# Two layers of attention and S4D convolution: staging the output weights elsewhere, new due times, one planner cost, tied additions and a reordered pool

## The chip, the cores and the metric

The kernel runs on one core of one Trainium2 chip. The metric is device time in microseconds (us) of one execution. Five engines work in parallel, each through its own instructions in their order: TensorE (PE), VectorE (DVE), ScalarE (ACT), GpSimd (POOL) and SyncE (SP). In this kernel SP issues most of the transfers and POOL the rest. The granted clock is the share of TensorE's full clock that the profile shows.

## The reference, cut to what matters

```python
def _A_ref(x, wqkv, wo):                     # S=2048, D=640, H=32 heads of 20
    qkv = (x @ wqkv)...                      # q, k, v per head
    scores = jnp.einsum("bhqd,bhkd->bhqk", q, k) * (Dh ** -0.5)
    p = _softmax(scores, axis=-1)
    o = jnp.einsum("bhqk,bhkd->bhqd", p, v)
    return o... @ wo
def _B_ref(u, log_A_real, A_imag, C_real, C_imag, log_dt, D_skip):
    dt = jnp.exp(log_dt)
    A = -jnp.exp(log_A_real) + 1j * A_imag   # 640 channels x 128 states
    C = (C_real + 1j * C_imag) * dt[:, None]
    P = jnp.exp((A * dt[:, None])[:, :, None] * pos[None, None, :])
    K = 2.0 * jnp.einsum("dn,dnl->dl", C, P).real      # one kernel of 2048 steps per channel
    ... y = irfft(rfft(u) * rfft(K))[:L]               # causal convolution
    return y + u * D_skip
x = x + _A_ref(_layernorm(x), ...)
x = x + _B_ref(_layernorm(x), ...)
x = x + _A_ref(_layernorm(x), ...)
x = x + _B_ref(_layernorm(x), ...)
```

## The kernel before, in words

The program is two layers, each an attention and then an output projection with the convolution. Both layers use the same weights and the same kernel K, so the generator of K and its transform run once, in layer 1.

**Attention.** The work is cut into 32 turns (8 groups of 4 heads by 4 blocks of 512 queries), each of 16 steps kt of 128 keys. A step makes two score tiles S on TensorE (`S<-qop,kop`), two exponentials of 128x1024 on ScalarE (`pt<-S`), and the products with the values (`pa<-pt,V`). At a turn's end VectorE gathers the block in `oc`, POOL sends its row of sums through DRAM (`dn<-oc`, `dr<-dn`), VectorE inverts them (`dr`), POOL spreads them again (`dn<-dr`, `db<-dn`), VectorE multiplies `oc` by `db`, and POOL stores `ot<-oc`. The very last block takes a way without DRAM (`m<-oc,dsel`, a reciprocal of `db`). A group change (turns 3, 7, 11 and so on) needs the next heads' operands, which SP loads (`kop<-ks`, `qop<-qs`, `qop<-qm`).

**What fills the gaps.** In layer 1 the same stretch also holds the q, k, v projections of the later groups (`m<-xh,wh`, emptied by VectorE into `qc`, split into `qhi`, `qlo`, stored to `qs` and `ks`; their weights `ws` split into `wh`, `wl`) and the generator `kgen` of K. For each of its 20 blocks POOL loads powers (`kpw<-wd`), VectorE's `expand` makes a table of them (`kpw`, `ktab`, `kwc`, `kwb`, `kdif`), VectorE makes the factors `ka` and `kb`, TensorE contracts them (`m<-kb,ka`, L335), VectorE empties `ko`, and POOL stores `kd<-ko`.

**What sets the order.** The program is written by a planner: class `Plan` keeps an estimated time of TensorE, ScalarE and VectorE (`plan.pe`, `plan.act`, `plan.dve`). Every VectorE operation adds its cost to `plan.dve`; a wait for a transfer adds nothing. `weave` emits the next piece of `kgen` where the plan has room, and the list `later` holds small steps, among them loads, each with a due time. While `plan.keep` is set, `tie` makes each instruction follow the one before on its engine; elsewhere a scheduler chooses the order, and `tie` is used where one operation shall follow another. Every engine then executes its list in order.

**The end of the first attention.** `end_jobs` runs when projections and generator are done. It calls `prefetch`, which opens the pools of the output projection, loads the output weights and puts the remaining loads into `rest`; these get due times from `plan.pe` on. `woh` and `wol` are the rounded half and the remainder of the weights:

```python
with tc.tile_pool(name="wos", bufs=NCT, side="right") as ws:
    for ct in range(NCT):
        wt = ws.tile([P, D], F32, name="wot")
        sy.dma_start(wt, wo[ct * P:ct * P + P, :])
        ge.tensor_copy(woh[:, ct, :], wt)
        ge.tensor_sub(wol[:, ct, :], wt, woh[:, ct, :])
```

**Output projection 1 and the kernel transform.** TensorE multiplies the rows `otl` (split into `oh`, `ol` by ScalarE and VectorE) with the weights into `po`, and VectorE adds `po` to `x` and takes statistics. `ktransform` runs between: for each of five blocks of 128 channels it loads `kl<-kd`, adds the skip to the first column (`kl<-kl,skip`, VectorE), transposes (`pkt<-ident,kl`), splits into `ktrh` and `ktrl`, multiplies by `e1s` (`pkx`), transposes and scales into `kxt` and makes `kn`. `kl0` holds its buffers; `kl0[3]`, called `kx1` or `kx`, is the one into which `pkx` is emptied.

**The convolution** (`ssm`) goes by rows of 128 positions: layer norm (`va`, `lt`, `rs`, `nb`, `u`, `uhx`, `ulx`), a transform (`psx<-uhx,e1s`, emptied into the pair `x1`, which the profile calls `x`, by a cast on ScalarE and a subtraction on VectorE), the product with the factors `ka`, `kb`, which SP loads, and the way back, for which SP loads `eb`. Buffers come from pools; where a pool takes memory that an earlier tile still holds, its first use waits for that tile.

Of the kernel before, what the change touches and what calls it, by code (L numbers as in the profile page):

```python
# [11 lines left out]
F32 = mybir.dt.float32  # L12
F32R = mybir.dt.float32r
F16 = mybir.dt.float16
# [73 lines left out]
def mha_s4d_kernel(ctx, tc, x_in, wqkv, wo, lar, aim, cr, ci, ldt, dsk,  # L88
# [109 lines left out]
    def kgen():  # L198
# [69 lines left out]
        def expand(k, w, tab, dif):  # L268

            while slow and slow[0][0] <= k:  # L270
                slow.pop(0)[1]()
            bs = slice(k * BC, k * BC + BC)
            lo = [tab[:, r, :, 0:24].rearrange("p d (g k) -> p d g k", k=8) for r in range(2)]
            hi = [tab[:, r, :, 24:28] for r in range(2)]
            for r in range(2):
                ve.tensor_mul(w[:, r], w[:, r], w[:, 2])
                a3 = w[:, r, 0:9, :].rearrange("p (g k) d -> p d g k", k=3)
                ve.tensor_copy(lo[r][:, :, :, 1:3], a3[:, :, :, 0:2])
                ve.tensor_copy(lo[r][:, :, :, 4:5], a3[:, :, :, 2:3])
                ve.tensor_copy(hi[r][:, :, 0:1], ld["ci" if r else "cr"][:, bs].unsqueeze(2))  # L280
                yield
            cm = [ld[n][:, bs].unsqueeze(2).to_broadcast([P, BC, 3]) for n in ("cr", "ci")]
            yield from cmul([a[:, :, 1:4] for a in hi], [w[:, r, 9:12, :].rearrange("p n d -> p d n") for r in range(2)], cm, [P, BC, 3], "kwc")
            yield from cmul([a[:, :, :, 3] for a in lo], [a[:, :, :, 1] for a in lo],
                            [a[:, :, :, 2] for a in lo], [P, BC, 3], "kwc")
            w4 = [a[:, :, :, 4:5].to_broadcast([P, BC, 3, 3]) for a in lo]
            yield from cmul([a[:, :, :, 5:8] for a in lo], [a[:, :, :, 1:4] for a in lo], w4, [P, BC, 3, 3], "kwb")
            ve.tensor_add(tab[:, 2], tab[:, 0], tab[:, 1])
            yield
            ve.tensor_sub(dif, lo[1][:, :, 0:3:2], lo[0][:, :, 0:3:2])  # L290
# [139 lines left out]
    def attention(x, stats):  # L430
# [521 lines left out]
        def end_jobs():  # L952

            while filler[0] is not None:
                while slot():
                    pass
                weave(1)
            if not first_layer:
                wx = sm.tile([P, 2], F32, name="wx")
                ve.reduce_max(wx[:, 0:1], wm, axis=AX.X)  # L960
                ge.partition_all_reduce(wx[:, 1:2], wx[:, 0:1], P, bass.bass_isa.ReduceOp.max)

                def bounds():
                    ve.tensor_max(flag[:, 0:1], flag[:, 0:1], wx[:, 1:2])
                    ve.reciprocal(wx[:, 0:1], wx[:, 1:2])
                    ve.tensor_scalar_mul(wx[:, 0:1], wx[:, 0:1], 2.0 ** -4)
                    ve.tensor_max(flag[:, 0:1], flag[:, 0:1], wx[:, 0:1])
                later.append((plan.pe + 6.0, bounds))
            qc_.close()
            if not first_layer:  # L970
                xpools.pop().__exit__(None, None, None)
            rest = []
            made = prefetch(x, rest)
            later.extend((plan.pe + 8.0 + (3.0 if first_layer else 4.0) * n, f) for n, f in enumerate(rest))
            later.sort(key=lambda e: e[0])
            return made

# [179 lines left out]
    def prefetch(x, rest):  # L1157
# [16 lines left out]
        if rest:  # L1174
            kl0[:] = [w1.tile([P, L], F32, name="kl"), w1.tile([P, NCT], F32, name="skip"),
                      w1.tile([P, 2, 32], F32, name="f2"), w1.tile([P, 4, NI // 2, 4, 32], F32, name="kx1"),
                      *(w1.tile([P, NI, P], F16, name=f"ktr{n}") for n in "hl"),
                      *(w1.tile([P, 4, 4, P], F32, name=f"kxt{n}") for n in range(2))]
            late[:] = [w1.tile([P, P], F32, name="dsel")]

            def small():
                sy.dma_start(kl0[1], dsk)
                sy.dma_start(late[0], c_dn)
                sy.dma_start(kl0[2], c_f2.rearrange("p (s m) -> p s m", s=2))
            rest[1:1] = small, lambda: load_kl(0)
            with tc.tile_pool(name="wos", bufs=NCT, side="right") as ws:
                for ct in range(NCT):
                    wt = ws.tile([P, D], F32, name="wot")
                    sy.dma_start(wt, wo[ct * P:ct * P + P, :])
                    ge.tensor_copy(woh[:, ct, :], wt)  # L1190
                    ge.tensor_sub(wol[:, ct, :], wt, woh[:, ct, :])
            rest.pop(0)()
            return x, c, woh, wol, c.enter_context(tc.tile_pool(name="wo2", bufs=2, side="right"))
        w2 = c.enter_context(tc.tile_pool(name="wo2", bufs=2, side="right"))
# [46 lines left out]
    def ktransform(e1):  # L1241

        c = ExitStack()
        c2 = c.enter_context(tc.tile_pool(name="f2", bufs=2))
        kl, skip, f2, x1, hi, lo, *xts = kl0

        def by_time(b, h):

            if h == 0:
                tie(ve.tensor_add(kl[:, 0:1], kl[:, 0:1], skip[:, b:b + 1]), None if b else late[1])  # L1250
            klv = kl.rearrange("d (p i) -> d i p", i=NI)
            for i4 in (2 * h, 2 * h + 1):
                pt = pst("X", [P, 4, P], F32, tag="X", name="pkt")
# [18 lines left out]
        def block(b):  # L1272

            def turned(t, xt, h):
                for q in (2 * h, 2 * h + 1):
                    pt = pst("X", [P, 4, P], F32, tag="X", name="pkt")
                    for g in range(4):
                        transpose(pt[:, g, :], of_group(x1, 16 * t + 4 * q + g), ident)
                    if q % 2:
                        ve.tensor_scalar_mul(xt[:, q], pt, ksc[:, 1:2])  # L1280
                    else:
                        se.activation(xt[:, q], pt, AF.Copy, scale=ksc[:, 1:2])

# [103 lines left out]
    def ssm(x, uh, ul, consts, last):  # L1387
# [18 lines left out]
        e1, f2, id16, fa = consts  # L1406
        with ExitStack() as c:
            c1 = c.enter_context(tc.tile_pool(name="s1", bufs=1))
            c2 = c.enter_context(tc.tile_pool(name="s2", bufs=2))
            c3 = c.enter_context(tc.tile_pool(name="s3", bufs=3))  # L1410
            order = {}

            def at(name, made):
# [36 lines left out]
                return px  # L1450

            def factors(m, ch):
                ka = c1.tile([P, 512], F32, bufs=5, name="ka")
                kb = c3.tile([P, 512], F32, name="kb")
                for t, src in ((ka, kha), (kb, khb)):
                    at("sp", sy.dma_start(t.rearrange("p (q k) -> p q k", k=P), src[m][:, ch]))
                return ka, kb

            def product(px, ka, kb, alone):
                t2 = c1.tile([P, 512], F32, name="t2")  # L1460
                at("dve", ve.stream_shuffle(t2, px, SWAP))
                at("dve", ve.tensor_mul(ka, px, ka))
                for f, *a in (("tensor_mul", kb, t2, kb), ("tensor_add", ka, ka, kb)):
# [35 lines left out]
                return add, after  # L1499

            def new_x1():
                return [c2.tile([P, 4, NI // 2, 4, 32], F16, name=f"x1{k}") for k in range(2)]

            x1 = new_x1()
            for i2 in range(8):
# [5 lines left out]
            for n in range(NQ + 15):  # L1511
# [3 lines left out]
                if n < NQ:  # L1515
                    if q == 0 and b:
                        x1 = nxt
                    if n % 4 == 0:
                        xt = c1.tile([P, 2, 4, 4, P], F16, name="xt")
                    stage2a(x1, q, xt)  # L1520
                if 2 <= n < NQ + 2:
                    ks[n - 2] = factors(*divmod(n - 2, 4))
# [258 lines left out]
```

## Time and profile before

| | us |
|---|---|
| three runs: median (lowest to highest) | 2665.14 (2664.39 to 2666.16) |
| the profiled execution | 2665.94 |
| its span in the profile | 2664.1 |
| busy: PE, DVE, ACT, POOL | 2492.7, 1517.5, 2342.6, 813.9 |
| granted TensorE clock, mean | 0.993 |

The stages of the span, read from the timeline: 0 to 116 us the layer norm, first projections and the generator's start; to 1093 attention 1; to 1290 output projection 1 with the kernel transform; to 1420 convolution 1; to 1488 the next layer norm and projections; to 2463 attention 2; to 2520 output projection 2; to 2664 convolution 2.

A row of a timeline reads: start, busy time, engine, line, operation, output<-inputs with shapes, how many, and in brackets the engine's idle time before it with what ended it. SPq is SP's transfer issue. Rows of the chain have start, length and what it was. Rows with a window in front list for each engine its busy time, then the granted clock, the share of the transfer engines and GB/s. L78 is the line of the helper through which tied instructions are issued.

### The profile page before, as it was taken

The page shows a single profiled execution, that of the slowest core. Times are in us where ns is not written, and L with a number is a line of the kernel's source. Part 1 is how long each engine was busy: PE and PEld are TensorE (multiplying, and loading weights), DVE is VectorE, ACT ScalarE, POOL GpSimd, SP SyncE. Part 2 cuts the span into 40 slices and gives each one's busy share as a digit, 9 for nine tenths or more (in the row PEclk, how much of TensorE's full clock was granted, in tenths as well). Part 3 has the DMA queues.
Part 4 walks back from the last instruction along what each step waited for, and adds up shares of the span by engine and source line. Part 5 has one row for each costly group of instructions (what it writes and reads, how often), then busy time and mean ns, then how long its engine had stood idle before and what let it go on. Part 6 is the DMA issues. An engine that isn't in the chain of part 4 may idle for free.

```text
span 2664.1 us, 118804 instructions
## 1 busy us (share of the span) xinstructions
PE 2492.7 (94%) x52388; PEld 1408.8 (53%) x52388; DVE 1517.5 (57%) x3417; ACT 2342.6 (88%) x2763; POOL 813.9 (31%) x1240
## 2 busy tenths in 40 slices
PE   7899999999999998799898999999999998999898
PEld 3445445444454443587796444454444443444798
DVE  7687778778855885376787333232232222143875
ACT  7899999999999999565765799999999999999474
POOL 1123334233332332311581122222222223222285
PEclk9999999999999999999999999999999999999999
DMA  6523222222222222454652121121121113222366
GB/s 208 185 52 85 60 78 71 77 57 74 56 60 51 51 69 76 168 204 164 213 175 72 41 58 51 50 60 47 43 67 38 51 32 91 69 67 57 124 201 183
DMA packets 186270, 241.99 MB, mean 91 GB/s; under 512 B 43408, under 2 KB 128720, under 8 KB 184080
## 3 DMA queue, kind: packets, MB, share of 16 engines
q1 hardware_dynamic: 150048, 188.28, 22.5%
q0 software_dynamic: 35696, 46.01, 7.4%
q8 instruction: 413, 6.77, 1.1%
q14 instruction: 113, 0.93, 0.1%
HBM read 158.16 MB, written 76.00 MB: 88 GB/s over the span
## 4 chain that ended last, share of the span: by engine, by line
ACT 58%; PE 19%; issue 10%; DVE 4%; DMA 4%; POOL 1%; SPq 0%; ACTq 0%; POOLq 0%; DVEq 0%
ACT pt L78 56%; PE psy L1417 3%; PE psv L1417 2%; PE pa L900 2%; PE po L193 2%; PE psx L1417 2%; PE S L866 1%; PE pst L1439 1%; PE pkx L193 1%; PE pkt L196 1%; PE m L618 1%; PE pq L771 1%; DVE x L78 1%; PE pkf L193 1%; DMA kl<-kd 0%
## 5 line engine op out<-in xcount | busy, mean ns | idle before, releaser
L78 ACT ACTIVATE pt<-S 128x1024 f32<-128x1024 f32 x2048 | 1927.3, 1033 | 32.9 <-PE S L866 20.3
L900 PE MATMUL pa<-pt,V 64*32 64x512 f32 x16384 | 1095.1, 590 | 0.2 <-DVE oc L78 0.2
L866 PE MATMUL S<-qop,kop 61*32 61x512 f16 x16384 | 874.7, 381 | 85.3 <-ACT pt L78 67.5
L866 PEld LDWEIGHTS <-kop 61*32 61x32 f16 x16384 | 365.8, 89 | 739.3 <-issue 620.1
L900 PEld LDWEIGHTS pa<-pt,V 64*32 64x32 f32 x16384 | 312.3, 106 | 68.6 <-issue 7.9
L78 POOL DMA_DIRECT2D dn<-oc x248 | 122.5, 501 | 595.3 <-DVE oc L78 575.8
L78 DVE TENSOR_SCALAR qc<-m 128x512 f32<-128x512 f32 (+1 forms) x68 | 46.8, 689 | 288.9 <-PE m L618 288.9
L78 POOL DMA_DIRECT2D db<-dn x248 | 125.1, 511 | 139.4 <-DMA dn<-dr 136.5
L78 DVE COPY oc<-pa 128x512 f32<-128x512 f32 x64 | 44.2, 691 | 195.1 <-PE pa L900 184.1
L78 POOL DMA_DIRECT2D ot<-oc x256 | 130.4, 516 | 81.2 <-DVE oc L78 53.8
L618 PE MATMUL m<-xh,wh 64*32 64x512 f16 x2560 | 144.4, 377 | 4.1 <-DVE qc L78 4.1
L618 PE MATMUL m<-xh,wl 64*32 64x512 f16 x2560 | 144.9, 377 | 0.0
L618 PE MATMUL m<-xl,wh 64*32 64x512 f16 x2560 | 143.5, 376 | 0.0
L78 ACT COPY xt<-pst 128x1024 f16<-128x1024 f16 x80 | 81.3, 1016 | 60.8 <-PE pst L1439 60.8
L618 PEld LDWEIGHTS <-wh 64*32 64x32 f16 x5120 | 90.4, 93 | 77.2 <-issue 34.6
L78 POOL DMA_DIRECT2D dn<-dr x62 | 34.5, 557 | 301.8 <-DVE dr L78 274.4
L1467 POOL TENSOR_TENSOR kb<-t,kb 128x512 f32<-128x512 f32 x76 | 97.2, 1279 | 66.8 <-DVE t L78 42.5
L78 DVE TENSOR_SCALAR V<-m 128x160 f32<-128x160 f32 x64 | 20.7, 324 | 161.8 <-PE m L584 161.8
L78 DVE TENSOR_TENSOR kb<-ktab 128x512 f32<-128x512 f32 x160 | 106.1, 682 | 0.0
L584 PEld LDWEIGHTS <-xh 128*128 128x128 f16 x960 | 79.4, 98 | 46.1 <-issue 30.3
L335 PEld LDWEIGHTS m<-kb,ka 128*32 128x32 f32 x3840 | 61.2, 110 | 74.1 <-issue 56.5
L1467 POOL TENSOR_TENSOR ka<-ka,kb 128x512 f32<-128x512 f32 x76 | 97.5, 1283 | 6.0
(312 smaller groups left out, 3945.1 us busy)
## 6 DMA issues: line engine op xcount, KB each, us to landing
ka<-kha SPq DMA_DIRECT2D x80, 256.0 KB
kb<-khb SPq DMA_DIRECT2D x80, 256.0 KB
db<-dn POOLq DMA_DIRECT2D x248, 64.0 KB, 3.3
kop<-ks SPq DMA_DIRECT2D x176, 80.0 KB
kpw<-wd POOLq DMA_DIRECT2D x60, 192.0 KB, 4.4
qop<-qs SPq DMA_DIRECT2D x256, 40.0 KB
ot<-oc POOLq DMA_DIRECT2D x256, 40.0 KB, 2.9
kha<-kn SPq DMA_DIRECT2D x20, 512.0 KB
```

Of the source, the lines that this page charges most:

```text
L78: made = f(out, *a, **k)
L193: chain(te.matmul(*a, **k))
L196: chain(te.transpose(*a, **k))
L335: chain(te.matmul(ps[32 * j:32 * j + 32, c8, :], a[n][:, ch, :], b[n][:, dd, :], start=(n == 0), stop=(n == 2), tile_position=(0, 32 * j)))
L584: chain(te.matmul(ps[:, :n], a_[:, ct, sl], m[:, ct, :], start=(k == 0), stop=(k == 14)))
L618: chain(te.matmul(ps[r][32 * t:32 * t + 32, :], a_[rows, ct, 32 * u:32 * u + 32], m[rows, ct, 512 * v:512 * v + 512], start=(k == 0), stop ...
L771: te.matmul(pq, a_[:, ct, :], m[:, ct, sl], start=(n == 0), stop=(n == 14))
L866: chain(te.matmul(S[32 * t:32 * t + 32, 512 * r:512 * r + 512], kt_[rows, kc + 32 * t:kc + 32 * t + 32], qt[rows, :], start=True, stop=Tru ...
L900: chain(te.matmul(pa[r][32 * j:32 * j + 32, :], V[rows, kt, VP * h:VP * h + 32], pts[j // 2][rows, 512 * (j % 2):512 * (j % 2) + 512], sta ...
L1417: at("pe", te.matmul(*a, **k))
L1439: at("pe", te.transpose(pt[:, k, g, :], of_group(x1[k], 4 * q + g), id16))
L1467: at("pool", getattr(ge, f)(*a))
```

## The change

Five edits:

1. In `expand`, for the first block only, 6.0 is added to `plan.dve` behind the first multiplication, which is the one that waits for the first powers.
2. In `prefetch` for layer 1, the weights are loaded into `kl0[3]` instead of a pool of their own, and VectorE makes `woh` and `wol` instead of POOL, one split for each entry of `rest`.
3. The due times of `rest` are 6.0 + 1.5 n behind `plan.pe` in layer 1 instead of 8.0 + 3.0 n. Layer 2 keeps its times.
4. In `ktransform`, the addition to `kl` of each later block is tied behind the last `kxt` that VectorE has written by then. Before, only the first was tied.
5. In `ssm`, the last convolution gets a pool of its own for `x1`, and `ka`, `t2` and `xt` move to a pool `s4`.

```diff
@@ expand
                 ve.tensor_mul(w[:, r], w[:, r], w[:, 2])
+                if k == r == 0:
+                    plan.dve += 6.0
@@ end_jobs
-            later.extend((plan.pe + 8.0 + (3.0 if first_layer else 4.0) * n, f) for n, f in enumerate(rest))
+            later.extend((plan.pe + (6.0 + 1.5 * n if first_layer else 8.0 + 4.0 * n), f) for n, f in enumerate(rest))
@@ prefetch
-            with tc.tile_pool(name="wos", bufs=NCT, side="right") as ws:
-                for ct in range(NCT):
-                    wt = ws.tile([P, D], F32, name="wot")
-                    sy.dma_start(wt, wo[ct * P:ct * P + P, :])
-                    ge.tensor_copy(woh[:, ct, :], wt)
-                    ge.tensor_sub(wol[:, ct, :], wt, woh[:, ct, :])
+            wt = kl0[3].rearrange("p c i s g -> p (c i s g)")[:, :NCT * D].rearrange("p (t d) -> p t d", t=NCT)
+
+            def split(ct):
+                ve.tensor_copy(woh[:, ct, :], wt[:, ct, :])
+                ve.tensor_sub(wol[:, ct, :], wt[:, ct, :], woh[:, ct, :])
+            for ct in range(NCT):
+                sy.dma_start(wt[:, ct, :], wo[ct * P:ct * P + P, :])
+                rest.append(lambda ct=ct: split(ct))
@@ ktransform
+        hold = [late[1]]
...
-                tie(ve.tensor_add(kl[:, 0:1], kl[:, 0:1], skip[:, b:b + 1]), None if b else late[1])
+                tie(ve.tensor_add(kl[:, 0:1], kl[:, 0:1], skip[:, b:b + 1]), hold[0])
...
-                        ve.tensor_scalar_mul(xt[:, q], pt, ksc[:, 1:2])
+                        hold[0] = ve.tensor_scalar_mul(xt[:, q], pt, ksc[:, 1:2]).ins
@@ ssm
+            if last:
+                cx = c.enter_context(tc.tile_pool(name="sx", bufs=2))
+            c4 = c.enter_context(tc.tile_pool(name="s4", bufs=1))
             c2 = c.enter_context(tc.tile_pool(name="s2", bufs=2))
             c3 = c.enter_context(tc.tile_pool(name="s3", bufs=3))
+            if not last:
+                cx = c2
...
-                ka = c1.tile([P, 512], F32, bufs=5, name="ka")
+                ka = c4.tile([P, 512], F32, bufs=5, name="ka")
...
-                return [c2.tile([P, 4, NI // 2, 4, 32], F16, name=f"x1{k}") for k in range(2)]
+                return [cx.tile([P, 4, NI // 2, 4, 32], F16, name=f"x1{k}") for k in range(2)]
```

What moves. VectorE at the start of the first attention, before: the end of the first block's table (`kwb`, `ktab`, `kdif`, `kbig`) and then the projection's `qc`.

```order
L78 TENSOR_TENSOR ktab<-kwb_1507,kwb_1508 128x32x3x3
L78 TENSOR_TENSOR ktab<-ktab 128x896
L78 TENSOR_TENSOR kdif<-ktab 128x512
L78 TENSOR_REDUCE kbig<-k_cr 128x1
L78 TENSOR_SCALAR qc<-m_1300 128x512
L78 SCALAR_TENSOR_TENSOR qc<-m_1301,qc 128x512
L78 TENSOR_TENSOR sq<-qc 128x512
```

The same engine and place after, from the table's first products (`kwc`) on:

```order
L78 TENSOR_TENSOR kwc_1591<-kpw_166,k_ci 128x96
L78 TENSOR_TENSOR kwc_1592<-kpw_166,k_cr 128x96
L78 TENSOR_SCALAR qc<-m_1300 128x512
L78 SCALAR_TENSOR_TENSOR qc<-m_1301,qc 128x512
L78 TENSOR_TENSOR sq<-qc 128x512
L78 CAST qhi<-qc 128x512
L78 TENSOR_TENSOR qlo<-qc,qhi 128x512
L78 TENSOR_SCALAR wh<-ws 128x640
L78 SCALAR_TENSOR_TENSOR wl<-ws,wh 128x640
L78 TENSOR_TENSOR ktab<-kwc_1591,kwc_1592 128x32x3
```

The projection's seven operations now stand in the middle of the table instead of behind it. All later pieces of the generator move too: on TensorE its first contraction goes from kt 13 to kt 24 and its last from kt 485 to kt 494 of the attention's 512; the `kpw` loads fall into other turns (11 and 23 get some that had none), and on SP, ahead of turn 7's end, the loads of `kop` and `qop` now stand ahead of one `ws` load and the `qs` stores instead of behind them.

POOL at the end of the first attention, before: turn 29's sums, the generator's last store (`kd<-ko`), the splits and turn 30's sums.

```order
L78 DMA dr<-dn 128x16
L78 DMA kd<-ko 128x8x64
L78 DMA dn<-dr 128x16
L78 DMA db<-dn 32x512 x4
L1190 CAST woh<-wot 128x640 x2
L1191 ISA
L1191 TENSOR_TENSOR wol<-wot,woh 128x640 x2
L1190 CAST woh<-wot 128x640 x2
L1191 TENSOR_TENSOR wol<-wot,woh 128x640 x2
L1190 CAST woh<-wot 128x640
L1191 TENSOR_TENSOR wol<-wot,woh 128x640
L78 DMA dn<-oc 16x1x32 x4
```

The same after, up to the output projection (`ul` is a layer norm's remainder):

```order
L78 DMA db<-dn 32x512 x4
L78 DMA kd<-ko 128x8x64
L78 DMA dn<-oc 16x1x32 x4
L78 DMA ot<-oc 20x512 x4
L78 DMA dr<-dn 128x16
L78 DMA dn<-dr 128x16
L78 DMA db<-dn 32x512 x4
L78 DMA ot<-oc 20x512 x8
L1235 ISA
L1235 TENSOR_TENSOR ul<-u,uh 128x640 x15
```

The splits are gone from POOL, and the instruction without a tile (ISA) stands ahead of `ul`. On VectorE the ten operations stand between turn 30's `oc` and the first `oh`, three tiles ahead of the inversion of `dr` and two behind it. On SP, `otl` now stands behind `x`, `skip`, `dsel` and `f`, ahead of `kl`.

VectorE at the last block of the kernel transform, before: the last `kxt` of a block, the emptying of `pkf` into `kn`, the addition to `kl`, and an addition to `x` with its statistics.

```order
L78 TENSOR_SCALAR kxt_25870<-pkt,ksc 128x512
L78 SCALAR_TENSOR_TENSOR ktrl<-pkt,ksc,ktrh 128x512 x2
L78 TENSOR_TENSOR x<-x,po 128x320
L78 COPY kn_27903<-pkf_27883 128x512
L78 BN_STATS st<-x 128x6
L78 COPY kn_27907<-pkf_27885 128x512
L78 TENSOR_TENSOR kl<-kl,skip 128x1
L78 TENSOR_TENSOR x<-x,po 128x320
```

The same addition after:

```order
L78 TENSOR_SCALAR kxt_25869<-pkt,ksc 128x512
L78 TENSOR_TENSOR ol<-otl,oh 128x640
L78 TENSOR_SCALAR kxt_25869<-pkt,ksc 128x512
L78 TENSOR_TENSOR kl<-kl,skip 128x1
L78 TENSOR_TENSOR x<-x,po 128x320
L78 BN_STATS st<-x 128x6
L78 SCALAR_TENSOR_TENSOR ktrl<-pkt,ksc,ktrh 128x512 x2
```

The addition has moved past the whole middle of the block, to just ahead of the `ktrl` that is made from it; the transpose of `kl` on TensorE stands where it stood. In the last convolution, two casts (ScalarE) and two subtractions (VectorE) of `x1` move from behind the last rows' `u` to between the `oh` casts of output projection 2, and SP loads four `ka` and three `kb` ahead of `eb` instead of behind it.

More of the change, by code (lines that the diff above doesn't have):

```diff
@@ L1459, in product @@
             def product(px, ka, kb, alone):
-                t2 = c1.tile([P, 512], F32, name="t2")
+                t2 = c4.tile([P, 512], F32, name="t2")
                 at("dve", ve.stream_shuffle(t2, px, SWAP))
@@ L1518, in ssm @@
                     if n % 4 == 0:
-                        xt = c1.tile([P, 2, 4, 4, P], F16, name="xt")
+                        xt = c4.tile([P, 2, 4, 4, P], F16, name="xt")
                     stage2a(x1, q, xt)
```

## The prediction

> **What bounds the kernel now.** I read the page's totals and its chain first, then the longest group, then, stage by stage, the waits of the engine that sets the pace there.
>
> ```profile
> span 2664.1 us, 118804 instructions
> ACT 58%; PE 19%; issue 10%; DVE 4%; DMA 4%; POOL 1%; SPq 0%; ACTq 0%; POOLq 0%; DVEq 0%
> L78 ACT ACTIVATE pt<-S 128x1024 f32<-128x1024 f32 x2048 | 1927.3, 1033 | 32.9 <-PE S L866 20.3
> ACT pt L78 <- PE S L866: 6.6, 6, 3.0
> ```
>
> ScalarE's 2048 exponentials carry 58% of the chain. They wait 32.9 us in the whole program; the last line (us, times, longest, from 139 to 1093 us) leaves 6.6 us of waits inside nearly all of the first attention. So no edit can make the attentions much shorter; time can only come out of single holes: one at the attention's start, one in its turn 7, one at its end, one in the kernel transform, one ahead of the last stage. The five edits go to these, and I price each hole.
>
> **1. The planner told of a load.** VectorE, then TensorE, then ScalarE at the start of the first attention, and the clock there:
>
> ```profile
> 123.54 0.56 DVE L78 TENSOR_TENSOR kpw<-kpw 128x384 f32<-128x384 f32 x1 [6.63 <-DMA kpw<-wd]
> 126.59 0.25 DVE L78 TENSOR_TENSOR kwc<-kpw,k_cr 128x96 f32<-128x96 f32 x1
> 133.99 0.68 DVE L78 TENSOR_SCALAR qc<-m 128x512 f32<-128x512 f32 x1
> 134.72 0.37 PE L618 MATMUL m<-xh,wh 64*32 64x512 f16 x1 [3.64 <-DVE qc L78]
> 137.43 1.02 ACT L78 ACTIVATE pt<-S 128x1024 f32<-128x1024 f32 x1 [5.13 <-PE S L866]
> 139.46 31.00 ACT L78 ACTIVATE pt<-S 128x1024 f32<-128x1024 f32 x33 [1.01 <-PE S L866]
> 135.00:140.00 5.00, 4.58 (x89) 2.37 (x95) 4.90 (x9) 1.56 (x2) 0.26 (x1) 0.66 0.13 30
> ```
>
> VectorE waits 6.63 us for the powers, runs the whole expansion, and only then empties the projection (qc at 133.99). TensorE stands for 3.64 us for that, works on at a granted clock of 0.66, and ScalarE loses 5.13 + 1.01 = 6.14 us. In the new order qc follows the kwc multiplication of 126.59 directly, so it starts near 126.8, 7.1 us earlier, more than the 6.14 us. The rest of the expansion (126.8 to 134.0) now runs beside exponentials; what waits for it is the generator's first contraction, and that moves from kt 13 to kt 24, which covers it. I take 5.5 us (3 to 6.1).
>
> The Trainium skill ("TensorE: Matmul & The Clock Gate", What's actually happening) says that the clock halves after an idle window of about 3.4 us and comes back after as long a busy one; the 3.64 us and the 0.66 agree.
>
> The generator's blocks now come about 17 us later (9 kt of two exponentials; 31.00 us for 33 in the row above are 0.94 us each), and so its loads meet other transfers. In turn 7, at a change of head group, before shows what such a meeting costs (SP, POOL, ScalarE):
>
> ```profile
> 348.47 0.32 SPq L78 DMA_DIRECT2D qs<-qhi  x1
> 357.98 3.35 POOL L78 DMA_DIRECT2D kpw<-wd  x3 [1.29 <-issue]
> 367.49 1.02 ACT L78 ACTIVATE pt<-S 128x1024 f32<-128x1024 f32 x1 [3.04 <-PE S L866]
> 369.06 1.02 ACT L78 ACTIVATE pt<-S 128x1024 f32<-128x1024 f32 x1 [0.55 <-PE S L866]
> 370.87 4.69 ACT L78 ACTIVATE pt<-S 128x1024 f32<-128x1024 f32 x5 [0.79 <-PE S L866]
> ```
>
> SP's queue sat behind qs<-qhi until 348.47, and the group's kop and qop loads went out only then, beside the kpw loads; ScalarE lost 3.04 + 0.55 + 0.79 = 4.4 us. In the new order the loads of kop and qop stand ahead of ws, qs and qs. But turn 7 keeps its kpw loads, and turns 11 and 23, which are also group changes, get some they did not have. I take a gain of 2 us (0 to 4.4); the new meetings are a rival.
>
> **2 and 3. Output weights split by VectorE, loads closer.** The end of the first attention, on SP, POOL, VectorE, ScalarE and TensorE:
>
> ```profile
> 1050.09 3.71 SPq L78 DMA_DIRECT2D wot<-in_wo  x5
> 1065.49 3.51 POOL L1191 TENSOR_TENSOR wol<-wot,woh 128x640 fp32r<-128x640 f32 x2 [8.76 <-issue]
> 1075.60 2.16 POOL L78 DMA_DIRECT2D dn<-oc  x4
> 1065.45 2.13 DVE L78 TENSOR_TENSOR oc<-oc,db 128x512 f32<-128x512 f32 x1
> 1087.80 0.17 DVE L78 TENSOR_SCALAR dr<-dr 128x16 f32<-128x16 f32 x1 [20.21 <-DMA dr<-dn]
> 1088.38 0.49 DVE L78 CAST oh<-otl 128x640 fp32r<-128x640 f32 x1
> 1088.91 0.83 DVE L78 TENSOR_TENSOR ol<-otl,oh 128x640 fp32r<-128x640 f32 x1
> 1088.56 0.56 POOL L78 DMA_DIRECT2D dn<-dr  x1 [7.33 <-DVE dr L78]
> 1093.99 0.69 DVE L78 TENSOR_TENSOR oc<-oc,pa 128x512 f32<-128x512 f32 x1
> 1103.61 0.69 DVE L78 TENSOR_TENSOR oc<-oc,db 128x512 f32<-128x512 f32 x1 [8.93 <-DMA db<-dn]
> 1106.14 3.34 DVE L78 RECIPROCAL db<-db 128x512 f32<-128x512 f32 x1
> 1095.91 0.73 ACT L78 CAST oh<-otl 128x640 fp32r<-128x640 f32 x1 [3.87 <-DMA otl<-ot]
> 1096.55 1.26 ACT L78 ACTIVATE ktrh<-pkt,ksc 128x512 f16<-128x512 f32 x2
> 1111.56 0.22 PE L193 MATMUL pkx<-ktrh,e1s 128*128 128x128 f16 x1 [2.57 <-DVE ktrl L78]
> 1136.36 2.78 POOL L1231 TENSOR_TENSOR ul<-u,uh 128x640 f16<-128x640 f32 x2 [23.32 <-ACT uh L78]
> ```
>
> oc of turn 30 gets its last addition just ahead of the multiplication of 1065.45 (an older block's), so it is ready near 1065.6, but its dn<-oc stands on POOL behind five splits and leaves at 1075.60. From there to db in VectorE's hands (1103.61) are 28.0 us. Without the splits it leaves near 1065.6, so db is there near 1093.6, before the last oc needs it (1093.99 + 0.69 = 1094.7). The 8.93 us of waiting goes.
>
> What is late next: ktrl needs ktrh, and ScalarE makes that (1096.55) after oh, which waits for otl until 1095.91. From the oc multiplication to pkx are 7.95 us now (1103.61 to 1111.56), among them the reciprocal's 3.34. Started at 1094.7 and held by ktrh until 1097.2, the same row of work takes two and a half more, with one ktrl ahead of the reciprocal: pkx near 1104.9 for 1111.56, 6.6 us earlier.
>
> The splits themselves are 5 x (0.49 + 0.83) = 6.6 us by the rows of oh and ol, and lie in VectorE's 20.21 us of idle time. Three stand ahead of dr's inversion, 4.0 us, done before dr lands. If that cover went, they would delay dr by 4.0. The 8.76 us ahead of the first split is a POOL instruction without a tile; it now stands ahead of ul, where POOL has 23.32 us to spare: free.
>
> Would VectorE's splits hold POOL's DMA issue? The dn<-dr of 1088.56 was issued beside the oh cast and the ol subtraction and took 0.56 us: no. The Trainium skill ("SBUF — State Buffer", Who interferes with whom) speaks against the change: VectorE and GpSimd share a port pair as an exclusive lock, and a VectorE copy starves descriptors for POOL's DMAs; by that rule each of four issues would wait for at most a copy, some 2 us in all, and the term would be 4.6. The stretched oc multiplication (2.13 us beside a POOL subtraction, 0.69 elsewhere) does show such a lock between the two engines' arithmetic, which the change removes.
>
> The transfers: the weights' load (1050.09) follows the generator's last block, so it leaves 17 us later, near 1067.
>
> ```profile
> wot<-in_wo SPq DMA_DIRECT2D x5, 320.0 KB
> x<-in_x_in SPq DMA_DIRECT2D x4, 1280.0 KB
> kl<-kd SPq DMA_DIRECT2D x2, 1024.0 KB
> otl<-ot SPq DMA_DIRECT2D x4, 320.0 KB
> 1095.00:1102.00 7.00, 1.87 (x9) 1.13 (x8) 0.00 (x0) 1.89 (x3) 1.76 (x4) 0.98 0.91 322
> ```
>
> The five weights, four x, one kl and two otl are 8,384 KB, 8.6 MB; at the 322 GB/s of the full queue 27 us, so otl lands near 1094, as before (1095.9). Closer due times serve to keep the queue that full. I take 6.5 us for the stage (3 to 9).
>
> **4. Additions tied.** TensorE, VectorE and the clock at the last block:
>
> ```profile
> 1209.47 0.16 DVE L78 TENSOR_TENSOR kl<-kl,skip 128x1 f32<-128x1 f32 x1 [3.87 <-DMA kl<-kd]
> 1210.08 0.70 PE L193 MATMUL po<-woh,ol 128*128 128x320 f32 x3 [2.93 <-DVE x L78]
> 1210.00:1216.00 6.00, 5.92 (x67) 3.97 (x68) 4.37 (x15) 3.23 (x6) 0.60 (x1) 0.72 0.06 24
> ```
>
> VectorE stood at kl with x's additions behind it, TensorE lost 2.93 us, and its clock of 0.72 over 6 us cost 1.7 more: 4.6. Tied behind the last kxt, kl comes when its load has landed; but then its transpose on TensorE waits for VectorE in each of four blocks, by about one queued operation of 0.5 to 0.8 us: 2.5. I take 2 us of gain (from 1 lost to 4.6 won).
>
> **5. Pools of the last stage.**
>
> ```profile
> 2514.48 0.23 PE L1417 MATMUL psx<-uhx,e1s 128*128 128x128 f16 x1 [4.96 <-DVE va L78]
> ```
>
> Two casts and two subtractions of x1, which stand now among the last row's steps on ScalarE and VectorE, go back to the oh casts of the out-projection, and the factors' loads precede eb. At the 0.7 and 0.8 us that such operations take above (oh, ol), that is up to 1.5 us on either engine, out of the last row's chain, or into a stage where VectorE is fuller. TensorE's 4.96 us wait is mostly the chain of row 14, which stays. I take 1.3 us (from 1.5 lost to 4 won, the most if the whole wait but a row's chain went).
>
> **Sum.** 5.5 + 2 + 6.5 + 2 + 1.3 = 17.3 us off the profiled 2665.9 us (span 2664.1 and 1.8 around it; the median is 0.8 below it): 2648.6. About 0.2%, 5.3 us, is what a measurement here can tell from no change.
>
> **Rivals.** A, the transfers take back the gain of the attention's end. They start 17 us later, and if otl lands at 1102.5, 6.6 us after the 1095.9 of now, pkx is where it was. The 8.6 MB then take 35.5 us, at 242 GB/s against the 322 of the row. Time: 17.3 - 6.5 = 10.8 off, 2655.1. Chance 0.15.
>
> B, the kpw loads that are new in turns 11 and 23 each make the 4.4 us stall of turn 7: 17.3 - 8.8 = 8.5 off, 2657.4. For it: the row of 357.98 lies in the stall. Against it: SP's new order sends kop and qop first. Chance 0.11.
>
> C, slower: the same late start, with transfers far from filling the engines. The other terms hold 10.8 us, so it is slower by more than 0.2% once pkx is 10.8 + 5.3 = 16.1 us late, at 1127.7, which is an otl near 1118.7 (9 us ahead, as 1104.9 is to 1095.9): 52 us for the 8.6 MB, 166 GB/s. At 150 GB/s, an estimate of under half the row's rate, they take 57 us, pkx comes at 1133, 21.4 us late, and the time is 2665.9 - 10.8 + 21.4 = 2676.5. Against it: the 322, and a kl and otl that leave as soon as SP's queue is free. Chance 0.07.
>
> D, the holes close and others of the same size open (TensorE at the tied additions, exponentials beside a later generator): within 5 us of now, 2664. Chance 0.07. The forecast has 0.60.
>
> **The numbers.** Its own range by the terms is 2641 to 2656; with A and B it reaches to 2660. Faster: 0.60 + 0.15 + 0.11 less 0.02 for A and B together: 0.84; same 0.08; slower 0.08.
>
> **What would show it.** Right: ScalarE without the 5.13 us wait near 132; dn<-oc of turn 30 on POOL within 2 us of oc, no wait for db, pkx 6 us sooner against the last exponential; no wait for kl over 2 us. Wrong: exponentials waiting at turns 11 or 23, oh waiting for otl past 1100, or TensorE waiting for kl in every block.

## The result and the profile after

The changed kernel takes 2649.89 us (median of 4, 2648.02 to 2652.04); before takes 2665.65 us (median of 4). The ratio is 0.9941, 95% interval 0.9924 to 0.9959: 15.8 us off, 11 to 20 by the interval. The forecast was 2648.6. The profiled execution after took 2652.04 us with a span of 2650.3.

The page's totals, the chain, the longest group, and ScalarE's waits from 116 to 1093 us (us, times, longest), of after; the last row is that of before for the same stretch:

```profile
span 2650.3 us, 118793 instructions
ACT 59%; PE 18%; issue 11%; DMA 4%; DVE 3%; POOL 1%; SPq 0%; ACTq 0%; POOLq 0%; DVEq 0%
L78 ACT ACTIVATE pt<-S 128x1024 f32<-128x1024 f32 x2048 | 1927.3, 1034 | 30.5 <-PE S L868 15.9
ACT pt L78 <- PE S L868: 6.9, 8, 2.3
ACT pt L78 <- PE S L866: 11.7, 7, 5.1
```

The exponentials' busy time is the same to the tenth, and no share of the chain differs from before by more than a point. What went lies in the holes. The start of attention 1 and its turns 7 and 11, ScalarE and the first `qc` on VectorE:

```profile
119.04 1.02 ACT L78 ACTIVATE pt<-S 128x1024 f32<-128x1024 f32 x1 [1.05 <-PE S L868]
121.18 1.02 ACT L78 ACTIVATE pt<-S 128x1024 f32<-128x1024 f32 x1 [1.11 <-PE S L868]
122.53 236.25 ACT L78 ACTIVATE pt<-S 128x1024 f32<-128x1024 f32 x252 [0.33 <-PE S L868]
358.93 125.11 ACT L78 ACTIVATE pt<-S 128x1024 f32<-128x1024 f32 x133 [0.15 <-PE S L868]
486.32 89.61 ACT L78 ACTIVATE pt<-S 128x1024 f32<-128x1024 f32 x95 [2.28 <-PE S L868]
792.94 293.08 ACT L78 ACTIVATE pt<-S 128x1024 f32<-128x1024 f32 x314 [0.73 <-PE S L868]
125.82 0.25 DVE L78 TENSOR_TENSOR kwc<-kpw,k_cr 128x96 f32<-128x96 f32 x1
129.22 0.69 DVE L78 TENSOR_SCALAR qc<-m 128x512 f32<-128x512 f32 x1 [3.15 <-PE m L620]
```

The 5.13 us hole is gone: `qc` now waits for TensorE, not TensorE for `qc`. Turn 7's stall is 0.15 us for 4.4. A stall of 2.28 us stands where turn 11 ends. The short waits at 119 to 122.5 us lie ahead of the place that edit 1 changes, and kernels without edit 1 have such waits too (1.05 us at 120.24 in only2, below). The last row says when the last exponential ends: 792.94 + 293.08 = 1086.0, against 1092.0 before.

The end of the attention on SP, POOL, VectorE, ScalarE and TensorE:

```profile
1059.16 2.55 SPq L78 DMA_DIRECT2D kx<-in_wo  x5
1058.80 0.69 DVE L78 TENSOR_TENSOR oc<-oc,pa 128x512 f32<-128x512 f32 x1
1059.78 1.96 POOL L78 DMA_DIRECT2D dn<-oc  x4 [3.26 <-DVE oc L78]
1066.63 0.82 DVE L78 TENSOR_TENSOR wol<-kx,woh 128x640 fp32r<-128x640 f32 x1
1066.91 0.58 POOL L78 DMA_DIRECT2D dr<-dn  x1 [3.04 <-DMA dn<-oc]
1072.94 0.43 DVE L78 CAST woh<-kx 128x640 fp32r<-128x640 f32 x1
1073.32 0.55 POOL L78 DMA_DIRECT2D dn<-dr  x1 [5.83 <-DVE dr L78]
1088.56 0.69 DVE L78 TENSOR_TENSOR oc<-oc,db 128x512 f32<-128x512 f32 x1
1091.36 3.34 DVE L78 RECIPROCAL db<-db 128x512 f32<-128x512 f32 x1
1088.09 0.72 ACT L78 CAST oh<-otl 128x640 fp32r<-128x640 f32 x1 [2.07 <-DMA otl<-ot]
1096.78 0.22 PE L193 MATMUL pkx<-ktrh,e1s 128*128 128x128 f16 x1 [3.48 <-DVE ktrl L78]
```

dn<-oc of turn 30 leaves 0.3 us behind its `oc` (10 before). The `oc` multiplication with `db` (1088.56) waits for nothing, and pkx begins 10.8 us behind the last exponential, where it was 19.5.

### The profile page after: what moved, and what is told of

Same layout as the page of the kernel before. It is cut to its first block, busy times and chain, and to the rows that moved or that the text cites. A ratio compares the mean times of both kernels' runs of the same rounds, so it can differ in the third digit from the quotient of the medians.

```text
span 2650.3 us, 118793 instructions
## 1 busy us (share of the span) xinstructions
PE 2490.3 (94%) x52388; PEld 1405.9 (53%) x52388; DVE 1518.5 (57%) x3427; ACT 2342.3 (88%) x2763; POOL 800.2 (30%) x1230
## 4 chain that ended last, share of the span: by engine, by line
ACT 59%; PE 18%; issue 11%; DMA 4%; DVE 3%; POOL 1%; SPq 0%; ACTq 0%; POOLq 0%; DVEq 0%
ACT pt L78 57%; PE psy L1427 2%; PE psv L1427 2%; PE po L193 2%; PE psx L1427 2%; PE pa L902 2%; PE pst L1449 1%; PE S L868 1%; DMA otl<-ot 1%; PE pkx L193 1%; DMA kop<-ks 1%; PE pv L586 1%; PE pkt L196 1%; PE pq L773 1%; PE pkf L193 1%
## 5 line engine op out<-in xcount | busy, mean ns | idle before, releaser
L78 DVE TENSOR_SCALAR V<-m 128x160 f32<-128x160 f32 x64 | 20.7, 323 | 162.8 <-PE m L586 162.8
```

The costliest lines, as they stand in the source:

```text
L78: made = f(out, *a, **k)
```

## The experiments

Each kernel below was profiled once and timed beside before on the same chip; the four kernels with one edit shared one chip, no1, no3, poolsplit and cost7 a second, no5, nokpw, laterecip and bothx a third. To compare stages between kernels I cut every trace at four events: A from the first exponential of attention 1 to the end of the last; B from there to the first `kx<-pkx` on ScalarE; C from there to the first `x<-psx` cast of convolution 1; D from there to the last such cast of convolution 2.

| kernel | edits | ratio to before (95%) | A | B | C | D |
|---|---|---|---|---|---|---|
| before | none | 1 | 976.0 | 20.7 | 163.0 | 1336.9 |
| only1 | 1 | 1.0030 (1.0019 to 1.0041) | 967.6 | 34.9 | 164.7 | 1338.1 |
| only2 | 2 | 0.9973 (0.9963 to 0.9982) | 977.4 | 13.4 | 163.1 | 1337.1 |
| only4 | 4 | 0.9987 (0.9976 to 0.9998) | 976.8 | 20.8 | 162.2 | 1337.7 |
| only5 | 5 | 0.9987 (0.9977 to 0.9997) | 975.4 | 20.8 | 164.0 | 1337.4 |
| after | all | 0.9941 (0.9924 to 0.9959) | 970.9 | 11.6 | 161.2 | 1338.6 |
| no1 | 2, 3, 4, 5 | 0.9950 (0.9936 to 0.9964) | 976.2 | 11.4 | 161.2 | 1335.9 |
| no3 | 1, 2, 4, 5 | 0.9940 (0.9926 to 0.9954) | 969.6 | 13.9 | 161.8 | 1336.8 |
| no5 | 1, 2, 3, 4 | 0.9933 (0.9919 to 0.9947) | 970.4 | 12.6 | 161.1 | 1336.2 |
| poolsplit | all, splits on POOL | 0.9972 (0.9963 to 0.9982) | 972.9 | 20.4 | 160.8 | 1338.7 |
| cost7 | all, 7.0 for 6.0 | 0.9942 (0.9928 to 0.9955) | 969.6 | 11.8 | 162.3 | 1334.2 |
| nokpw | all, powers later | 0.9946 (0.9931 to 0.9961) | 975.6 | 11.5 | 162.8 | 1335.2 |
| laterecip | all, one more tie | 0.9928 (0.9914 to 0.9941) | 973.6 | 11.0 | 162.1 | 1334.5 |
| bothx | both of these | 0.9941 (0.9926 to 0.9956) | 972.6 | 10.5 | 161.3 | 1337.7 |

D, which holds the whole of attention 2, varies by 4.5 us with no relation to any edit, so the end-to-end time of one trace doesn't tell a hole of 2 us. Of the stages, B is the one that does: it lies within 0.1 us in before, only4 and only5, and within 1.2 us in after, no1, no5, cost7 and nokpw. C lies within 2.0 us in the kernels with edit 4, A within 2.0 without edit 1 and within 6.0 with it and the powers' loads in their places; there I use means.

**only1.**

```diff
                 ve.tensor_mul(w[:, r], w[:, r], w[:, 2])
+                if k == r == 0:
+                    plan.dve += 6.0
```

> Edit 1 alone. Theory (each edit works in its own hole): ScalarE's 5.13 us hole after 132 us shrinks to under 3 us and the 4.4 us stall at turn 7's end goes, as in the changed kernel; a stall of about 2.3 us appears at turn 11's end, where the new powers' loads meet the group's loads. Attention 1 ends about 6 us earlier; the end of the attention (db, pkx) keeps its wait of 8 to 9 us for db. Time about 2659.5, 6 off. Rival (the edits need each other: the generator's later end makes the weights on POOL later still, and the end loses what the front gains): 2663 to 2666.

Attention 1 is shorter by 8.4 us, the largest gain in A of all, and the kernel is slower by 0.30%, 8 us. POOL, ScalarE and VectorE at the end of its attention:

```profile
1055.73 0.51 POOL L78 DMA_DIRECT2D dn<-oc  x1 [3.26 <-DVE oc L78]
1068.77 1.54 POOL L1193 TENSOR_TENSOR wol<-wot,woh 128x640 fp32r<-128x640 f32 x1 [8.58 <-issue]
1078.93 1.21 POOL L78 DMA_DIRECT2D dn<-oc  x2
1099.34 0.72 ACT L78 CAST oh<-otl 128x640 fp32r<-128x640 f32 x1 [17.37 <-DMA otl<-ot]
1107.41 0.69 DVE L78 TENSOR_TENSOR oc<-oc,db 128x512 f32<-128x512 f32 x1 [14.86 <-DMA db<-dn]
```

The generator ends later, so the weights arrive later, and POOL's splits (behind 8.58 us at the instruction without a tile) hold the last two of turn 30's dn<-oc until 1078.93, only 3 us before the last exponential ends (1082.0). `otl`'s load leaves SP only at 1079.04, with the splits done, and ScalarE waits 17.37 us for it. The wait that ends last is VectorE's for `db`: 28.5 us from 1078.93 to 1107.41, as the 28.0 in before. The rival of the expectation is right, and stronger than it said: without edit 2, edit 1 loses 14.2 us in B for its 8.4 in A.

**only2.** Edit 2 as in the change, with the due times of before:

```diff
-                    ge.tensor_copy(woh[:, ct, :], wt)
-                    ge.tensor_sub(wol[:, ct, :], wt, woh[:, ct, :])
+            for ct in range(NCT):
+                sy.dma_start(wt[:, ct, :], wo[ct * P:ct * P + P, :])
+                rest.append(lambda ct=ct: split(ct))
```

> Edit 2 alone, with the old due times 8 + 3 n. Theory (POOL's queue was the cause): dn<-oc of turn 30 leaves POOL within 2 us of oc, no wait for db after the last exponential, pkx 6 to 9 us sooner against the last exponential: 2657 to 2660. Rival (the closer due times are the cause): the first otl lands too late with the old ones, ScalarE's oh waits for it, and the gain is 0 to 3 us: 2662 to 2666.

B falls by 7.3 us and the time by 0.27%, 7 us. With the due times of before the gain is there, so the closer times aren't its cause; poolsplit, below, asks whether the engine is. Two splits now stand between the last `oc` and the reciprocal on VectorE:

```profile
1096.27 0.69 DVE L78 TENSOR_TENSOR oc<-oc,db 128x512 f32<-128x512 f32 x1
1096.87 0.49 DVE L78 CAST woh<-kx 128x640 fp32r<-128x640 f32 x1
1097.93 0.82 DVE L78 TENSOR_TENSOR wol<-kx,woh 128x640 fp32r<-128x640 f32 x1
1102.04 3.35 DVE L78 RECIPROCAL db<-db 128x512 f32<-128x512 f32 x1
```

**no3.** The due times alone are taken back:

```diff
-            later.extend((plan.pe + (6.0 + 1.5 * n if first_layer else 8.0 + 4.0 * n), f) for n, f in enumerate(rest))
+            later.extend((plan.pe + 8.0 + (3.0 if first_layer else 4.0) * n, f) for n, f in enumerate(rest))
```

> All edits but the third: due times 8 + 3 n. Theory (the due times only place the last two splits): two of the five splits come behind the last oc on VectorE, 2.6 us, and pkx moves by about 2: 2652. Rival A (with the generator 17 us later the loads need the closer times): oh waits for otl as in edit 1 alone, 5 us or more, and the time is 2655 or more. Rival B (nothing but order): 2650.

B is 13.9 us against 11.6, as only2's 13.4 is against no1's 11.4: by these traces the closer times are worth 2.0 to 2.3 us, by the place of two splits; kernels that share after's splits differ by 1.2 us in B. The ratio, 0.9940 against 0.9941, doesn't show it, and the interval is wider than 2 us. Rival A, that `oh` waits 5 us or more for the loads, falls.

**poolsplit.** The engine, or the place in the queue?

```diff
             def split(ct):
-                ve.tensor_copy(woh[:, ct, :], wt[:, ct, :])
-                ve.tensor_sub(wol[:, ct, :], wt[:, ct, :], woh[:, ct, :])
+                ge.tensor_copy(woh[:, ct, :], wt[:, ct, :])
+                ge.tensor_sub(wol[:, ct, :], wt[:, ct, :], woh[:, ct, :])
```

> The changed kernel, but POOL makes the five splits, still as steps of rest with their due times and from the same buffer, so that the sums of turn 30 leave ahead of them. It asks whether the engine or the place in POOL's queue made the gain. If the place ahead of the sums alone: within 1 us of the changed kernel, 2650. If the splits on POOL are the trouble wherever they stand among turn 30's transfers (dn<-dr and db<-dn behind 9 us of a POOL instruction and 11 us of splits): db comes 8 to 12 us after the last oc, and the time is 2657 to 2661.

The sums leave at once, and it gains nothing at the end: B is 20.4 us. POOL and VectorE:

```profile
1062.25 1.96 POOL L78 DMA_DIRECT2D dn<-oc  x4 [3.26 <-DVE oc L78]
1080.94 3.05 POOL L1192 TENSOR_TENSOR wol<-kx,woh 128x640 fp32r<-128x640 f32 x2 [9.69 <-issue]
1084.62 0.74 POOL L78 DMA_DIRECT2D dn<-dr  x1
1091.22 2.02 POOL L78 DMA_DIRECT2D db<-dn  x4
1099.79 0.69 DVE L78 TENSOR_TENSOR oc<-oc,db 128x512 f32<-128x512 f32 x1 [8.67 <-DMA db<-dn]
```

`dr` was inverted at 1075.25, but its way back, dn<-dr, leaves POOL at 1084.62 behind 9.69 us at the same instruction and the splits, and db<-dn behind the rest of them. The wait for `db` is 8.67 us, where before had 8.93. Two of the four steps, dn<-oc and dr<-dn (1069.27), are ahead of the splits now; that buys nothing while the other two, dn<-dr and db<-dn, stand among and behind them. So POOL's queue was the cause of the wait for `db`, and taking the splits off POOL is what removes it.

The trace settles a second thing, the place of the weights, which edit 2 changes too. SP's wait and its first `otl` load in before, then that load in after, then `oh` on ScalarE in poolsplit:

```profile
SPq L78 <- POOL wol L1191: 16.9, 1, 16.9
1075.68 0.38 SPq L78 DMA_DIRECT2D otl<-ot  x1
1065.15 0.55 SPq L78 DMA_DIRECT2D otl<-ot  x1
1089.09 0.72 ACT L78 CAST oh<-otl 128x640 fp32r<-128x640 f32 x1 [0.61 <-DMA otl<-ot]
```

In before the pool of `otl` is opened on the side where `wos` has just been closed, and SP waits 16.9 us for POOL's `wol`. With the weights in `kl0[3]` they don't: in poolsplit `otl` leaves SP at 1068.35, ahead of the first split, and `oh` waits 0.61 us for it. So edit 2 opens two queues: the engine frees POOL's, the place frees SP's. No kernel has VectorE's splits from the old place, so what SP's part is worth by itself isn't known.

**no1.** Edit 1's three lines are left out of the change.

```diff
-                if k == r == 0:
-                    plan.dve += 6.0
```

> All edits but the first. Theory (edit 1 is worth its holes in attention 1 once POOL's queue is free at the end): ScalarE's 5.13 us hole and turn 7's 4.4 us are back, turn 11 runs through, and the end of the attention is as short as in the changed kernel, 10.5 us from the last oc to the first kx: 6 us slower than the changed kernel, 2656. Rival (edit 1's later generator costs at the end whatever the queue): at or below the changed kernel's time, 2648 to 2651.

A is 976.2 again and B stays at 11.4, so with the other edits there edit 1 costs nothing at the end and its worth is to be read from A: the five kernels without it have 975.4 to 977.4, a mean of 976.4; the seven with it and the powers' loads in their places 967.6 to 973.6, a mean of 970.7: 5.7 us. The times alone don't show that much: no1's median, 2652.85 us, is 3 us above after's, less than the 6 expected, and the intervals overlap.

**only4.** The ties alone:

```diff
-                tie(ve.tensor_add(kl[:, 0:1], kl[:, 0:1], skip[:, b:b + 1]), None if b else late[1])
+                tie(ve.tensor_add(kl[:, 0:1], kl[:, 0:1], skip[:, b:b + 1]), hold[0])
```

> Edit 4 alone. Theory: VectorE's 3.87 us wait for kl's load in the last block goes and TensorE's 2.93 us behind it with its low clock; in each block the transpose of kl may wait up to 0.8 us. Net 2 us off: 2663.5. Rival (the transposes' waits take all of it back): 2665 to 2667.

0.9987, 3.5 us off with 0.5 to 6.4 in the interval; but only5, whose edit shows no worth below, has the same ratio. By stage C, the four kernels without edit 4 have a mean of 163.7 us, the ten with it 161.7: 2.0 us. Only4 itself has 162.2, 0.8 us below before and 0.9 to 2.5 below the three others on its chip, and no kernel has all edits but this one, so these traces put the edit at 0.8 to 2.5 us. VectorE waits for `kl` nowhere in after; two of its additions, and on TensorE the transposes that read the first:

```profile
1112.12 0.15 DVE L78 TENSOR_TENSOR kl<-kl,skip 128x1 f32<-128x1 f32 x1
1176.94 0.14 DVE L78 TENSOR_TENSOR kl<-kl,skip 128x1 f32<-128x1 f32 x1
1112.37 1.14 PE L196 MATMUL pkt<-ident,kl 128*128 128x128 f32 x8 [0.32 <-issue]
```

Two of TensorE's waits in the transform of after (us, times, longest):

```profile
PE pkt L196 <- ACT kxt L78: 3.5, 2, 2.3
PE po L193 <- DVE x L78: 0.5, 2, 0.2
```

Before has the first of these with the same numbers, and 3.4 us with a longest of 2.9 for the second: that hole is gone. The profile's list of waits names none of TensorE for `kl`, but the rows show one. In each of the four blocks the transposes begin 0.10 us behind the end of the addition; ahead of the first three TensorE stands for 0.32, 0.34 and 0.86 us (at 1112.37, 1145.58 and 1177.18), which the profile puts down to issue and to `oh`. That is 1.5 us that the tie costs.

**only5 and no5.** The pools alone, and everything but the pools:

```diff
+            if last:
+                cx = c.enter_context(tc.tile_pool(name="sx", bufs=2))
+            c4 = c.enter_context(tc.tile_pool(name="s4", bufs=1))
```

> Edit 5 alone. Theory: TensorE's hole before the last row of output projection 2 shrinks by about 1 us and the end moves with it: 2664.4. Rival (the new order of the factors' loads delays the last products on POOL by 1.4 us, as the changed kernel's trace has it at the end): 2665.5, no gain.

> All edits but the fifth. Theory from the traces so far (from the first x1 cast of convolution 1 to the last of convolution 2 the kernels with edit 5 take 1334 to 1339 us, those without 1337 to 1338): edit 5 is worth nothing that can be told apart, and the time is that of the changed kernel, 2649 to 2652. Rival (the prediction's 1.3 us, or the 2.9 of edit 5 alone by its runs): 2652 to 2654.

only5 is 0.13% faster by its runs, yet the kernel without edit 5 is no slower than the one with it (0.9933 against 0.9941). D has a mean of 1336.6 us in the nine kernels with edit 5 and 1337.2 in the five without, and what is left of the span behind D 51.2 and 51.6. What the edit was priced on, TensorE's hole ahead of the last row, stands in after, and in no5:

```profile
2501.38 0.27 PE L1427 MATMUL psx<-uhx,e1s 128*128 128x128 f16 x1 [4.79 <-DVE x L78]
```

```profile
2497.70 0.29 PE L1422 MATMUL psx<-uhx,e1s 128*128 128x128 f16 x1 [4.96 <-DVE va L78]
```

So the hole is the same length, 4.79 against 4.96 us. Whether the edit is worth a microsecond elsewhere stays open.

**cost7.**

```diff
-                    plan.dve += 6.0
+                    plan.dve += 7.0
```

> The changed kernel with 7.0 instead of 6.0 added to the plan. The plan then has no powers' load in turn 11, but some in turns 15 and 23, and the generator's last contraction is at kt 484 instead of 495. If loads of powers in a group-change turn are what stalls it: turn 11's 2.3 us go, and turn 15 or 23 shows a like stall; between 2648 and 2652. If the earlier end of the generator is worth something at the attention's end: below 2647. If the plan's spots matter by chance: any time within 5 us of the changed kernel.

The powers' loads went out in the same turns as in after (turn 11's at 470.78, in after at 471.78) and turn 11's stall was 2.18 us, so, against the expectation, the plan did not move and this run is a repeat of after: 0.9942. It tells nothing of its question.

**nokpw.** Is it the powers' loads that stall turn 11?

```diff
-                later.extend((plan.dve + n, lambda: slow and slow.pop(0)[1]()) for n in (18.0 + wait, 21.0 + wait, 24.0 + wait))
+                later.extend((plan.dve + n, lambda: slow and slow.pop(0)[1]()) for n in (18.0 + wait, 21.0 + wait, 24.0 + wait) if qb != 2)
```

> The changed kernel, but the powers' loads are not taken from their list in the turns that end with a group change; they go out a turn later. Theory (in turn 11 these loads lengthen the transfers that the end of the turn waits for): the 2.2 us stall at turn 11's end, which every kernel with edit 1 has shown, goes; 2 us off, 2648. Rival (the stall comes from the order of VectorE's and SP's steps at that place, whatever POOL loads): it stays, 2650.

No load of powers is left in turn 11 (POOL goes from db<-dn at 468.95 straight to dn<-oc at 484.88), and the stall is still there. Its ScalarE rows at turns 11 and 28:

```profile
486.06 59.68 ACT L78 ACTIVATE pt<-S 128x1024 f32<-128x1024 f32 x63 [2.23 <-PE S L868]
1006.17 1.02 ACT L78 ACTIVATE pt<-S 128x1024 f32<-128x1024 f32 x1 [4.68 <-PE S L868]
```

Its chain (start, length, what) ahead of the first and of the second:

```profile
481.00 0.69 DVE qlo L78
481.69 0.50 DVE vh L78
...
483.12 0.69 DVE oc L78
...
985.66 5.82 DMA kpw<-wd
...
991.58 0.57 DVE kpw L78
...
1002.23 0.61 DVE oc L78
```

So the stall of turn 11 is no meeting of transfers: by this chain VectorE empties and splits a projection (qc to vh) ahead of the turn's `oc`, and TensorE waits for `oc`. No run takes the projection away from there. The powers that were put off arrived just ahead of an expansion, and from 991.58 to 1002.23 the whole expansion ran ahead of turn 28's `oc`: a new 4.68 us hole, of the same kind as the one that edit 1 removed.

**laterecip and bothx.** In after the reciprocal of the last block stands ahead of two of the four ktrl that pkx needs. One more tie puts it behind them:

```diff
-            ve.reciprocal(db, db)
+            inv[:] = [ve.reciprocal(db, db)]
...
+                if b == 0 and i4 == 3:
+                    tie(inv[0], made.ins)
```

> The changed kernel with one more tie: the reciprocal of the last block's sums (3.34 us on VectorE) behind the last ktrl of the transform's first block. Theory (after edits 2 and 3 the reciprocal and the two steps with it are what stands ahead of pkx): from the last exponential to the first kx 8 to 9 us instead of 11.6, and as the last block's rows are wanted only late, 2 to 3 us off: 2647. Rival (the last block's rows or its stores become late, or pkx waits for something else): 2650 or more.

> Both of the above in one kernel. If both theories hold, 4 to 5 us off the changed kernel: 2645. If one holds, 2647 to 2648.

laterecip, VectorE and then TensorE:

```profile
1098.18 0.74 DVE L78 SCALAR_TENSOR_TENSOR ktrl<-pkt,ksc,ktrh 128x512 f16<-128x512 f32 x1
1098.84 3.34 DVE L78 RECIPROCAL db<-db 128x512 f32<-128x512 f32 x1
1100.33 0.23 PE L193 MATMUL pkx<-ktrh,e1s 128*128 128x128 f16 x1 [2.34 <-DMA e1s<-in_c_e]
```

pkx now waits for the matrix e1s, whose load is issued only when the attention ends, and B falls by 0.6 us, not 3, which is within what B varies. Its median, 2647.93 us (0.9928), is the lowest here, but the interval overlaps that of after. bothx adds nokpw's edit, 0.9941.

## Why the prediction was right, step by step

**Edit 1, 5.5 us at the start and 2 in turn 7.** The trace of after has 2.5 us of waits at the start for 6.14, and 0.15 for 4.4 in turn 7, so 3.6 and 4.2; turn 11 and some smaller waits give back 3. Over the kernels of stage A's means, ScalarE's waits without edit 1 and with it are 5.9 and 1.5 us at the start, 4.3 and 0.4 in turn 7, none and 2.2 in turn 11: 4.4 + 3.9 - 2.2 = 6.1, near the 5.7 that A gives for the 7.5 of the sum. So turn 7 was priced too low, and the step that failed is that the sum put turn 11 at nothing. The start was priced 1.1 us too high: its hole is gone, and what stays are the short waits ahead of the changed place. `qc` doesn't start near 126.8 but waits for TensorE until 129.22, and no exponential waits for it. Turn 7's stall goes in every kernel with edit 1. The reason given fits, as the group's loads left at 341.24 in after, for 349.61 before, but the exponentials are ahead there too, and no run tests that order alone.

**Rival B** was wrong in its mechanism. A stall at turn 11 came, but nokpw shows it without the powers' loads, and turn 23, which also got some, shows none of this size. A wait at turn 11 was one of the prediction's own signs of being wrong, and it came; it took 2.2 us, not 4.4 twice.

**Edits 2 and 3, 6.5 us.** Mis-sized: B fell by 9.1 us, just outside the 3 to 9. The step that failed is the 2.5 us for ktrl held by ktrh. The prediction has `otl` land near 1094 by its 27 us, and yet holds ktrl by before's ktrh, which follows an `otl` of 1095.9. It did not see why that one was so late: SP had stood 16.9 us for POOL's splits, which edit 2's place for the weights ends. In after `otl` landed soon enough for ScalarE's ktrh to be there 0.2 us behind the `oc` multiplication, and from that to pkx were 8.2 us (1088.56 to 1096.78), as in before's 7.95. The loads began 26.9 us ahead of the last exponential's end and `otl` was there 2.1 us behind it, 29 us for the 27 of the estimate; rivals A and C, late loads, fall. POOL's issues beside VectorE's splits took 0.58 and 0.55 us (1066.91, 1073.32), as without them. These two lie almost wholly beside subtractions; the dr<-dn of after that lies longest beside a cast, 0.42 us from 764.08 on, took 0.57. The lock that the Trainium skill describes ("SBUF — State Buffer", Who interferes with whom), which would have made the term 4.6, is not seen on these issues.

**Edit 4, 2 us.** Stage C: 2.0 by the means, with 0.8 to 2.5 by the single traces. The wait of 2.93 us is gone, and the transposes wait for `kl` as the prediction said, 1.5 us in all where it took 2.5. TensorE waiting for `kl` in every block was one of its signs of being wrong; it waits in three of four, inside the price.

**Edit 5, 1.3 us.** Not there. The step that failed is that two casts and subtractions fewer in the last row's chain shorten the hole: it waits for `x` now, 4.79 us, instead of `va`.

**The sum.** 5.7 + 9.1 + 2.0 + 0 is 16.8, for 17.3 forecast; the runs say 15.8 (11 to 20). That the total is so close is in part luck: edits 1 and 5 were priced 1.8 and 1.3 us too high, edits 2 and 3 were priced 2.6 too low, and these cancel. One assumption under the sum was wrong and did no harm: that the edits' worths add. Edit 1 alone costs 8 us; its gain is only there with POOL's queue free at the end. The prediction had the generator's later end among the transfers (rivals A and C) and missed it on POOL, where the change removed the cost in the same step.

## What to carry to other kernels

When work is moved later to close a hole, follow the last piece of it to the stage's end and see what is queued behind it on every engine: here a gain of 8 us became a loss of 8, until another edit freed that queue. A round trip through DRAM is as late as its last issue, so work on the engine that issues it belongs behind all four steps or on another engine, not among them. Where a buffer is staged decides which loads wait for its last reader: look for that wait on the loading engine before pricing the transfers. Price a hole by what ends next to it, not by what is taken out of its chain: edit 5's hole and laterecip's were both filled at once by the next wait.

## What the runs showed of the hardware

Ahead of the first subtraction of the splits, where POOL's order has an instruction without a tile, POOL stood for 8.76 us in before, 8.58 in only1 and 9.69 in poolsplit, and the profile names nothing that it waited for. Ahead of `ul` in after it is not seen: POOL is idle there for 23.86 us and waits for `uh`. And the stretch D took 1334.2 to 1338.7 us over the kernels, 4.5 us of difference that goes with none of the edits.
